# Capped attention and two feed-forward layers: the attention's waits re-ordered, the first inverse root moved from ScalarE and VectorE to a small Newton chain on GpSimd

## The chip, the core and the metric

The kernel runs on one core of one Trainium2 chip. The metric is device time in microseconds (us), lower is better. Before the change three runs took 539.45, 539.74 and 539.93 us, a median of 539.74 us. One further execution was profiled: it took 540.45 us, of which its instructions span 538.7 us. All times read below, and all positions ("at 69.76"), are microseconds from the start of that span.

The engines are named as the profile names them: PE is TensorE's matmul (PEld its weight load), DVE is VectorE, ACT is ScalarE, POOL is GpSimd, SP is SyncE, which here only issues DMAs.

## What is computed

```python
def _attn_ref(q, k, v, cap):                       # 2 batches x 12 heads x 448 x 64, float32
    scores = scale * np.matmul(q, k.transpose(0, 1, 3, 2))
    scores = cap * np.tanh(scores / cap)
    attn = np.exp(scores - np.max(scores, axis=-1, keepdims=True))
    attn = attn / (np.sum(attn, axis=-1, keepdims=True) + 1e-09)
    return np.matmul(attn, v)

def _moe_ref(x, w_gate, w_val, w_out, rms_g):      # 896 tokens, 768 wide, 1536 inside
    rms = np.sqrt(np.mean(x * x, axis=-1, keepdims=True) + 1e-06)
    xn = x / rms * rms_g
    g = xn @ w_gate
    return (g / (1.0 + np.exp(-g)) * (xn @ w_val)) @ w_out

def _moe2_ref(x, w_in, w_out, alpha):              # 896 tokens, 768 wide, 2048 inside
    h = x @ w_in
    return (np.maximum(h, 0.0) + alpha * np.minimum(h, 0.0)) @ w_out
```

The three are applied one after the other. The change touches how the attention is ordered and how 1/rms is made for the first of the two batches.

## The kernel before

Tokens lie along the free axis (448 per batch), features along the partitions. The attention goes through twelve head pairs, one in each pass of a loop `for i in range(NPAIR)`; below, "pass 9" is the pass with i = 9. Every instruction is put on its engine's queue in the order in which the code is written, and each engine works its queue strictly in that order, so the code order is the schedule. Tiles come from pools; a tile whose pool has no free buffer waits until the last reader of the buffer's previous tile is done.

What pass i puts on PE: the last 64 keys' scores of pair i (`qk_tail`, L219), three groups of six score matmuls (`qk`, L229), then the work of the pair before, i-1: its tail products and row sums (`sums`, L272 and L290), and its products with the values (`pv`, L256). In passes 4, 6, 8 and 10 two matmuls (`spread`, L373) also bring the inverse row sums of two earlier pairs to all partitions. ACT does the tanh of four score tiles (L240) and one long exp (L243) in a pass.

DVE serves all others: it copies finished outputs out of PSUM (`evac_o`, `ee`, L320) and row sums (`evac_u`, `us`, L328), which SP then lays out as 64 rows of 28 values (`gt`, L331). `recip` (L338 to L343: `gf`, `th`, `tl`) inverts these and two SP DMAs send them back as rows (`r`, L346). DVE also splits the queries and keys of the next pair in a high and a low part (`prep`: `hi` L195, `lo` L196) and decodes weights for the first layer (`w_bits` L122, `w_lo` L143, some of `w_hi` L137). Lists named `first` and `second` (filled by `a(...)` and `z(...)`) hold, per pass, what is issued behind `soft(i)` and at the pass's end. POOL has the squares for the mean square (`square`, L353 to L361) and sums of weight blocks (`sum1` to `sum4`, L130).

Two PSUM pools matter: `ps_o` (tag "o") and `ps_r` (tag "u") have one buffer each. The outputs `oo` of a pair, one of the two `spread` results, and the mean square `ms` of a batch share "o" in turn. The first batch's mean square is made in pass 9 by one matmul with ones (`rms_sum`, L398) of what POOL accumulated in six squares; DVE copies it to `spare` (L572), ACT takes the root of its mean (L405), which loads another table before and again behind it, and DVE inverts it in pass 10 (L408). The last pass' row sums and outputs (`us`, `oo`) share one PSUM tile.

Behind the attention both layers multiply 2 x 2 blocks by seven products (`P1` to `P7`) in slots; hooks `do(n, rank, fn)` put the work of ACT, DVE and POOL behind slot n, ordered by rank. `osplit` and `osplit_low` (L672 on DVE) split the operands of the first layer's output product, whose matmuls are L796.

Of the kernel before, what the change touches and what calls it, by code (L numbers as in the profile page):

```python
# [12 lines left out]
U32 = mybir.dt.uint32  # L13
AF = mybir.ActivationFunctionType
# [3 lines left out]
P = 128  # L18
# [39 lines left out]
def attn_moe_kernel(ctx: ExitStack, tc: tile.TileContext, units, qk_in, v, sel, w, gvec, alpha, out):  # L58
# [23 lines left out]
    r2 = [aconst.tile([P, S], F32R, name=f"r2_{i}") for i in range(2)]  # L82

# [193 lines left out]
    def sums(i):  # L277

        t = pt[i]
        if i == last:  # L280
            both = ps_s.tile([P, 2, 512], F32, tag="s", name="us")
            us[i], oo[i] = both[:, 0], both[:, 1]
        else:
            us[i] = under()
            if i:
                oo[i] = upper("oo")

        def add(h, x, k, m=slice(0, P), src=None):
            q = h + 2 * x
            nc.tensor.matmul(  # L290
                us[i][q * Q:q * Q + Q, HALF[0]], ones[m, :Q], t[m, k, src or HALF[x]], start=k == 2 * TG,
                stop=k // 2 == TG - 1, skip_group_check=True,
            )

        pv_tail(i, False)
        for h in range(2):
            for x in range(2):
                if split[i]:
                    add(h, x, 2 * TG, HEAD[x], HALF[h])
                else:  # L300
                    add(h, x, 2 * TG, HEAD[h])
        if i == 0 and split[i]:
            pv_tail(i, True)
        for n in range(2 * TG):
            for x in range(2):
                add(n % 2, x, n)
        if i and split[i]:
            pv_tail(i, True)
# [101 lines left out]

    oper = {}
# [56 lines left out]
    with tc.manual_schedule():  # L468
# [8 lines left out]
        for t in r2:  # L477
            nc.vector.memset(t.bitcast(F32), 0.0)
# [34 lines left out]
        def a(i, fn, *args):  # L513
            first.setdefault(i, []).append((fn, args))
# [3 lines left out]

        conv = conv_seq[:]
# [6 lines left out]
        for i in range(NPAIR):  # L526
# [6 lines left out]
            if i % 2 == 1 and i > 2:  # L533
                steps.insert(i < 9, (recip, (i - 3) // 2))
            for step in steps:
                a(i, *step)
            if i - 2 in range(len(conv)):
                a(i, w_bits, conv[i - 2])
                if i - 2 < len(conv) - RAW:
                    a(i, w_next, conv[i - 2])  # L540
# [8 lines left out]
        a(9, rms_root, 0)  # L549
# [4 lines left out]
        for put, n, fn, g in ((z, 6, sum1, 0), (z, 7, sum1, 1), (z, 7, sum2, 0), (a, 8, sum2, 1), (a, 8, sum3, 0),  # L554
                              (z, 8, sum3, 1), (z, 10, sum4, 0)):
            put(n, fn, "g", g)
        z(10, rms_tail, 0)
        a(11, xnorm, K3)
        z(11, xnorm, K3 + 1)
        for i in range(NPAIR):  # L560
# [8 lines left out]
            if i == 9:  # L569
                rms_sum(0, upper("ms"))  # L570
                rms_keep(0)
                nc.vector.tensor_copy(rstd[0], ms_of[0][:, :S])  # L572
                ms_of[0] = rstd[0]
            two = lambda: ps_s.tile([P, 2, 512], F32, tag="s", name="s")
            for g in range(TG - 1):
                qk(i, g, two())
                if pairs and i != 8 and g == 0:
                    norms(i - 4, under(), upper("rps"))
                if (i, g) == (1, 0):
                    oo[0] = upper("oo")  # L580
                    pv(0, range(2))
# [5 lines left out]
            if i == 10:  # L587
                sums(i - 1)
# [5 lines left out]
            if i and i != 10:  # L594
                sums(i - 1)
            if i == 1:
                evac_o(0)
            if i:
                evac_u(i - 1)
                if i > 1:  # L600
                    pv(i - 1)
                del pt[i - 1], hi[i - 1], lo[i - 1], vt[i - 1]
# [472 lines left out]
        for way, p, js, hi_at, lo_at in (  # L1075
# [5 lines left out]
            for h, j in enumerate(js):  # L1081
                do(o0 + hi_at[h], 0.2, osplit, way, p, j, h)
                do(o0 + lo_at[h], 2.2, osplit_low, way, p, j, h)
# [264 lines left out]
```

## Time and profile before

| what | value |
|---|---|
| median of three runs | 539.74 us |
| profiled execution: time, span | 540.45 us, 538.7 us |
| PE busy in the span | 530.2 us (98%) |
| PEld, DVE, ACT, POOL busy | 451.1, 448.2, 400.6, 112.0 us |
| PE busy from 60 to 80 us, from 80 to 100 us | 18.35, 19.16 us of 20 each |
| PE busy from 100 to 200 us, from 300 to 500 us | 100.0 us, 200.0 us |
| mean granted TensorE clock | 0.999 |

The attention takes the first hundred microseconds; behind it PE is hardly ever without work. So what the change can move lies in PE's holes of the first hundred microseconds, and in one hole behind them. An engine's busy time includes the time in which an instruction has begun and is held up, so a long instruction on DVE or POOL is compared with its usual length before it is called work. In a row of the timeline the first two columns are the start and the duration, both in us, x is the number of instructions, and what stands in brackets is the idle time before it with what ended it.

### The profile page before, as it was taken

To read this page: it belongs to the slowest core of one execution; us is meant where nothing else is said; L and a number is where in the kernel's file an instruction comes from. 1 tells how busy PE (TensorE), PEld (TensorE's weight loads), DVE (VectorE), ACT (ScalarE), POOL (GpSimd) and SP (SyncE) were. 2 spreads that over 40 slices of the span, in tenths; PEclk is the share of its full clock that TensorE was granted. 3 is DMA by queue.
4 is the path that set the end of the run, shared out by engine and by line. 5 is a ranking of instruction groups with operands and counts; after the bars stand their busy time and mean duration, and the time that the engine had idled before them with its cause. 6 is when DMAs were issued, how large, how long until landed. Compare 5 with 4: busy or idle time off the path is not lost.

```text
span 538.7 us, 8345 instructions
## 1 busy us (share of the span) xinstructions
PE 530.2 (98%) x3322; PEld 451.1 (84%) x3322; DVE 448.2 (83%) x516; ACT 400.6 (74%) x475; POOL 112.0 (21%) x80
## 2 busy tenths in 40 slices
PE   8999999999999999999999999999999999999997
PEld 5554544699999999999998999999999999999996
DVE  5588889798999968689779796869997897998951
ACT  7989989476766665477688776789989996995530
POOL 0023763300066441010013011110210231210000
PEclk9999999999999999999999999999999999999999
DMA  6856520400344426047865759433466789564111
GB/s 214 317 168 230 179 76 11 159 19 2 102 133 175 161 90 219 0 176 250 273 179 101 157 196 308 80 58 125 169 235 225 215 226 205 98 145 111 51 52 51
DMA packets 22343, 80.05 MB, mean 149 GB/s; under 512 B 3744, under 2 KB 6688, under 8 KB 22304
## 3 DMA queue, kind: packets, MB, share of 16 engines
q1 hardware_dynamic: 16378, 65.43, 35.4%
q0 software_dynamic: 5552, 13.70, 13.9%
q8 instruction: 26, 0.43, 0.3%
q10 hardware_dynamic: 374, 0.39, 0.2%
q14 instruction: 13, 0.11, 0.1%
HBM read 62.99 MB, written 2.75 MB: 122 GB/s over the span
## 4 chain that ended last, share of the span: by engine, by line
PE 88%; DVE 5%; ACT 3%; POOL 2%; DMA 1%; issue 1%; DVEq 0%; SPq 0%; ACTq 0%
PE s L450 19%; PE x L450 13%; PE m L450 13%; PE s L826 8%; PE x L826 7%; PE x L796 5%; PE s L796 5%; PE m L826 4%; PE m L796 3%; PE s L229 2%; PE oo L256 2%; PE rps L290 2%; PE s L462 1%; ACT pt L243 1%; DVE wt L122 1%; PE oo L272 1%
## 5 line engine op out<-in xcount | busy, mean ns | idle before, releaser
L143 DVE TENSOR_TENSOR wl<-wt,wh 128x768 fp32r<-128x768 f32 x109 | 111.5, 1024 | 21.2 <-ACT wh L137 20.8
L137 ACT CAST wh<-wt 128x768 fp32r<-128x768 f32 x106 | 87.7, 830 | 39.7 <-PE s L826 9.2
L130 POOL TENSOR_TENSOR wt<-wt 128x768 f32<-128x768 f32 x25 | 58.4, 2341 | 164.7 <-DVE wl L143 75.7
L117 ACT CAST top<-raw 128x768 f16<-128x768 bf16 x64 | 68.9, 1077 | 21.1 <-DMA raw<-w_in 11.6
L122 DVE SCALAR_TENSOR_TENSOR wt<-raw,top 128x768 uint32<-128x768 uint32 x64 | 66.8, 1045 | 1.0 <-ACT top L117 1.0
L450 PE MATMUL s<-xx,wh 128*128 128x448 f32 x264 | 63.6, 365 | 0.0
L672 DVE TENSOR_TENSOR xx<-b,xx 128x896 fp32r<-128x896 f32 (+1 forms) x55 | 62.1, 1135 | 0.0
L450 PEld LDWEIGHTS s<-xx,wh 128*128 128x128 f32 x264 | 49.3, 187 | 4.8 <-issue 0.9
L450 PE MATMUL x<-xx,wh 128*128 128x448 f32 x204 | 49.9, 366 | 0.0
L450 PE MATMUL m<-xx,wh 128*128 128x448 f32 x204 | 49.5, 364 | 0.0
L893 POOL DMA_DIRECT2D wt<-wt x25 | 21.6, 864 | 126.6 <-DVE wt L122 62.0
L240 ACT ACTIVATE pt<-s,cinv 128x896 f32<-128x896 f32 (+1 forms) x48 | 40.8, 910 | 5.0 <-PE s L229 2.4
L450 PEld LDWEIGHTS x<-xx,wh 128*128 128x128 f32 x204 | 38.2, 188 | 3.5 <-issue 0.4
L450 PEld LDWEIGHTS m<-xx,wh 128*128 128x128 f32 x204 | 38.3, 188 | 3.0
L826 PE MATMUL s<-xx,wh 128*128 128x448 f32 x144 | 40.5, 362 | 0.0
L826 PE MATMUL x<-xx,wh 128*128 128x448 f32 x128 | 36.0, 362 | 0.0
L243 ACT ACTIVATE pt<-pt,cap_t 128x3136 f32<-128x3136 f32 (+2 forms) x13 | 35.2, 2711 | 0.4
L450 PE MATMUL s<-xx,wl 128*128 128x448 f32 x132 | 33.8, 364 | 0.0
L796 PE MATMUL s<-xx,wh 128*128 128x448 f32 x108 | 30.4, 362 | 0.0
L826 PEld LDWEIGHTS s<-xx,wh 128*128 128x128 f32 x144 | 27.0, 187 | 2.3
L796 PE MATMUL x<-xx,wh 128*128 128x448 f32 x96 | 27.3, 363 | 0.6 <-DVE xx L672 0.6
L256 PE MATMUL oo<-pt,vt 128*32 128x448 f32 x264 | 27.1, 540 | 0.4 <-ACT pt L243 0.4
(208 smaller groups left out, 1124.7 us busy)
## 6 DMA issues: line engine op xcount, KB each, us to landing
raw<-w_in SPq DMA_DIRECT2D x68, 768.0 KB
wt<-wt POOLq DMA_DIRECT2D x25, 384.0 KB, 5.3
rw<-qk_in SPq DMA_DIRECT2D x11, 480.0 KB
vt<-v_in SPq DMA_DIRECT2D x12, 288.0 KB
lent<-wt POOLq DMA_DIRECT2D x5, 384.0 KB, 7.0
b<-b POOLq DMA_DIRECT2D x4, 448.0 KB, 5.3
out<-P SPq DMA_DIRECT2D x5, 224.0 KB
out<-b SPq DMA_DIRECT2D x2, 448.0 KB
```

The lines of the kernel that those rows point to most:

```text
L117: copy(top_of[u].bitcast(F16)[:, 1::2], raw_t[u].bitcast(BF16)[:, 4:4 * n + 4:4])
L122: nc.vector.scalar_tensor_tensor(out=f_t[u].bitcast(U32), in0=raw_t.pop(u).bitcast(U32)[:, 1:2 * n + 1:2], scalar=13, in1=top_of.pop(u), o ...
L130: add(out=t, in0=f_t[a], in1=f_t[b], op=op)
L137: copy(h_t[u], f_t[u].rearrange("p (k m) -> p k m", m=P))
L143: nc.vector.tensor_tensor(out=l_t[u], in0=f_t[u].rearrange("p (k m) -> p k m", m=P), in1=h_t[u], op=ALU.subtract)
L240: nc.scalar.activation(out=part, in_=st.pop((i, g)), func=AF.Tanh, scale=cinv)
L243: nc.scalar.activation(out=t[:, done:to], in_=t[:, done:to], func=AF.Exp, scale=cap_t)
L256: nc.tensor.matmul(oo[i][q * Q:q * Q + Q, :S], vv[:, n, q % 2 * Q:q % 2 * Q + Q], t[:, n, :], start=i == c == 0, stop=i > 0 and c == TG - ...
L450: nc.tensor.matmul(ps[:, r, :S], lhs, rhs, start=first and n == 0, stop=n == len(mm) - 1, skip_group_check=True,)
L672: nc.vector.tensor_tensor(out=out, in0=a, in1=b, op=op)
L796: nc.tensor.matmul(dst[m], wt[:, kk * MB + m, :], x, start=first and u == 0 and kk == 0 and n == 0, stop=u == UO - 1 and kk == 1 and n == ...
L826: nc.tensor.matmul(dst[m], wt[:, kk * MB + m, :], x, start=first and u == kk == i == 0, stop=last and kk == 1 and i == 2, skip_group_check ...
```

## The change

There are six edits.

1. `recip` now stands ahead of `prep` in passes 3, 5 and 7 too.
2. In passes 4, 6 and 8 the row sums of the pair before are copied out (and their DMAs issued) ahead of the weight decoding instead of behind it.
3. One weight sum on POOL (`sum2` of block 0) moves from ahead of the squares of pass 8 to behind them.
4. The first mean square: its matmul goes behind the first score group of pass 9. Instead of the copy to `spare`, ACT's root and DVE's inversion, DVE copies 32 rows to `mrow` at the end of the list `first[9]`, SP lays one row out as 16 x 28 values, POOL scales them, DVE makes a first guess of the inverse root with two integer operations, POOL runs four Newton steps of four operations and splits the result in two parts, four SP DMAs write them as rows of `rr`, and in pass 11 a matmul with `sel_t` spreads them; DVE copies that to `spare`.
5. In pass 10 the row sums go back behind all three score groups; in the last pass `us` and `oo` have a PSUM tile each.
6. In the first layer's output product the low part of one operand (`P6`, first half) is made one slot earlier and ranked ahead of more of the other work.

```diff
-            both = ps_s.tile([P, 2, 512], F32, tag="s", name="us")
-            us[i], oo[i] = both[:, 0], both[:, 1]
+            us[i], oo[i] = (ps_s.tile([P, 2, 512], F32, tag="s", name=x)[:, 0] for x in ("us", "oo"))
...
+    def root_begin(ms):
+        u = sb.tile([Q, S], F32, tag="sq", name="mrow", bufs=2)
+        nc.vector.tensor_copy(u, ms[:Q, :S])
+        nc.sync.dma_start(out=tiny_tile("x"), in_=u[:1].rearrange("h (p s) -> h p s", p=RP))
+
+    def root_small():
+        x, y, t = small["x"], tiny_tile("y"), tiny_tile("t")
+        ts, mul = nc.gpsimd.tensor_scalar, lambda o, a, b: nc.gpsimd.tensor_tensor(out=o, in0=a, in1=b, op=ALU.mult)
+        ts(out=x, in0=x, scalar1=1.0 / DM, scalar2=RMS_EPS, op0=ALU.mult, op1=ALU.add)
+        nc.vector.tensor_scalar(
+            out=t.bitcast(U32), in0=x.bitcast(U32), scalar1=1, scalar2=None, op0=ALU.logical_shift_right
+        )
+        nc.vector.tensor_scalar(
+            out=y.bitcast(I32), in0=t.bitcast(I32), scalar1=-1.0, scalar2=float(0x5F3759DF), op0=ALU.mult, op1=ALU.add
+        )
+        for _ in range(4):
+            mul(t, y, x)
+            mul(t, t, y)
+            ts(out=t, in0=t, scalar1=-0.5, scalar2=1.5, op0=ALU.mult, op1=ALU.add)
+            mul(y, y, t)
+        th, tl = tiny_tile("th", F32R), tiny_tile("tl", F32R)
+        nc.gpsimd.tensor_copy(th, y)
+        nc.gpsimd.tensor_tensor(out=tl, in0=y, in1=th, op=ALU.subtract)
+        for r0, part in enumerate((th, tl)):
+            for r in (r0, r0 + Q):
+                nc.sync.dma_start(
+                    out=rr[r:r + 1].rearrange("r (p s) -> r p s", p=RP).bitcast(F32), in_=part.bitcast(F32)
+                )
+
+    def root_end(ps):
+        nc.tensor.matmul(ps[:, :S], sel_t[:D], rr, start=True, stop=True, skip_group_check=True)
+        rms_keep(0)
+        nc.vector.tensor_copy(rstd[0], ps[:, :S])
...
+        EARLY = (4, 6, 8)
...
-                steps.insert(i < 9, (recip, (i - 3) // 2))
+                steps.insert(0, (recip, (i - 3) // 2))
             for step in steps:
                 a(i, *step)
             if i - 2 in range(len(conv)):
+                if i in EARLY:
+                    a(i, sums, i - 1)
+                    a(i, evac_u, i - 1)
                 a(i, w_bits, conv[i - 2])
...
-        a(9, rms_root, 0)
+        a(9, lambda: root_begin(ms_of.pop(0)))
+        z(9, root_small)
...
-        for put, n, fn, g in ((z, 6, sum1, 0), (z, 7, sum1, 1), (z, 7, sum2, 0), (a, 8, sum2, 1), (a, 8, sum3, 0),
+        for put, n, fn, g in ((z, 6, sum1, 0), (z, 7, sum1, 1), (a, 8, sum2, 0), (a, 8, sum2, 1), (a, 8, sum3, 0),
                               (z, 8, sum3, 1), (z, 10, sum4, 0)):
             put(n, fn, "g", g)
-        z(10, rms_tail, 0)
...
-            if i == 9:
-                rms_sum(0, upper("ms"))
-                rms_keep(0)
-                nc.vector.tensor_copy(rstd[0], ms_of[0][:, :S])
-                ms_of[0] = rstd[0]
...
+                if (i, g) == (11, 0):
+                    root_end(upper("rps"))
+                if (i, g) == (9, 0):
+                    rms_sum(0, upper("ms"))
...
-            if i == 10:
-                sums(i - 1)
             if i:
                 qk(i, TG - 1, third())
...
-            if i and i != 10:
+            if i and i not in EARLY:
                 sums(i - 1)
...
-                evac_u(i - 1)
+                if i not in EARLY:
+                    evac_u(i - 1)
...
-            (2, "P5", (4, 4, 0), (2, 3, 5), (4, 5, 6)), (0, "P6", (5, 5, 0), (5, 6, 8), (8, 8, 9)),
+            (2, "P5", (4, 4, 0), (2, 3, 5), (4, 5, 6)), (0, "P6", (5, 5, 0), (5, 6, 8), (7, 8, 9)),
...
-                do(o0 + lo_at[h], 2.2, osplit_low, way, p, j, h)
+                do(o0 + lo_at[h], 1.5 if (p, h) == ("P6", 0) else 2.2, osplit_low, way, p, j, h)
```

What stands in DVE's queue in pass 9 before the change, from the copy of pair 7's output (`ee`) to the copy of pair 8's row sums (`us`); `spare` is the copy of the mean square `ms`, `gf` to `tl` is `recip`, `hi` and `lo` are pair 10's:

```order
L320 COPY ee_958<-oo_916 128x448
L572 COPY spare_967<-ms_965 128x448
L338 TENSOR_SCALAR gf_1000<-gt_836,eps_t_87 64x28
L339 RECIPROCAL gf_1000<-gf_1000 64x28
L342 CAST th_1003<-gf_1000 64x28
L343 TENSOR_TENSOR tl_1004<-gf_1000,th_1003 64x28
L195 CAST hi_1009<-rw_896 128x832
L196 TENSOR_TENSOR lo_1010<-rw_896,hi_1009 128x832
L122 SCALAR_TENSOR_TENSOR wt_1013<-raw_703,top1_94 128x768
L328 COPY us_1043<-rps_1016 128x224
```

The same place after the change; `mrow` is now the copy that frees the PSUM buffer of `ms`, and `t` and `y` are the first guess:

```order
L321 COPY ee_960<-oo_906 128x448
L339 TENSOR_SCALAR gf_1000<-gt_838,eps_t_87 64x28
L340 RECIPROCAL gf_1000<-gf_1000 64x28
L343 CAST th_1003<-gf_1000 64x28
L344 TENSOR_TENSOR tl_1004<-gf_1000,th_1003 64x28
L197 CAST hi_1009<-rw_897 128x832
L198 TENSOR_TENSOR lo_1010<-rw_897,hi_1009 128x832
L124 SCALAR_TENSOR_TENSOR wt_1013<-raw_735,top1_95 128x768
L421 COPY mrow_1015<-ms_974 32x448
L329 COPY us_1046<-rps_1019 128x224
L429 TENSOR_SCALAR t_1063<-x_1017 16x28
L432 TENSOR_SCALAR y_1062<-t_1063 16x28
```

The copy out of `ms` moved from ahead of `recip` to behind `recip`, `prep` and the decoding of a weight block.

POOL's queue before, from the first block's S2 sum to the third weight sum behind the squares (`s2` is the accumulated square, `wt` a weight block):

```order
L130 TENSOR_TENSOR wt_312<-wt_754,wt_312 128x768
L357 TENSOR_TENSOR sq_906<-xf_95 128x448
L361 TENSOR_TENSOR s2_546<-s2_546,sq_906 128x448
L357 TENSOR_TENSOR sq_909<-xf_95 128x448
L361 TENSOR_TENSOR s2_546<-s2_546,sq_909 128x448
L130 TENSOR_TENSOR wt_406<-wt_853,wt_406 128x768
L130 TENSOR_TENSOR wt_500<-wt_701,wt_312 128x768
L130 TENSOR_TENSOR wt_605<-wt_807,wt_406 128x768
```

POOL's queue after, the same stretch up to the first operation on the small tile `x`:

```order
L358 TENSOR_TENSOR sq_937<-xf_96 128x448
L362 TENSOR_TENSOR s2_548<-s2_548,sq_937 128x448
L358 TENSOR_TENSOR sq_940<-xf_96 128x448
L362 TENSOR_TENSOR s2_548<-s2_548,sq_940 128x448
L132 TENSOR_TENSOR wt_314<-wt_756,wt_314 128x768
L132 TENSOR_TENSOR wt_408<-wt_855,wt_408 128x768
L132 TENSOR_TENSOR wt_532<-wt_733,wt_314 128x768
L132 TENSOR_TENSOR wt_607<-wt_809,wt_408 128x768
L428 TENSOR_SCALAR x_1017<-x_1017 16x28
```

One weight sum changed sides: four of them now stand in a row between the last square and the small chain.

PE's queue in pass 9 after the change, from the tail scores (L221) to the first matmul into pair 8's `oo`:

```order
L221 MATMUL s<-rw 64x224 x4
L231 MATMUL s<-hi 128x448 x2
L231 MATMUL s<-hi,lo 128x448 x2
L231 MATMUL s<-lo,hi 128x448 x2
L399 MATMUL ms<-s_548,ones 128x448
L231 MATMUL s<-hi 128x448 x2
L231 MATMUL s<-hi,lo 128x448 x2
L231 MATMUL s<-lo,hi 128x448 x2
L231 MATMUL s<-hi 128x448 x2
L231 MATMUL s<-hi,lo 128x448 x2
L231 MATMUL s<-lo,hi 128x448 x2
L274 MATMUL oo<-pt,vt 32x224 x4
```

The matmul into `ms` moved behind the first of the three score groups; the next tile in its buffer is still `oo`.

## Rows read from the trace of the kernel before

**Rows 1.** The page: PE's busy tenths in 40 equal slices of the span.

```profile
PE   8999999999999999999999999999999999999997
```

**Rows 2.** Timeline of PE, passes 7 and 8: start, duration, line, tiles, [idle before].

```profile
53.33 0.61 PE L219 MATMUL s<-rw 64*64 64x224 f32 x8
...
60.35 0.61 PE L219 MATMUL s<-rw 64*64 64x224 f32 x8
61.52 0.47 PE L373 MATMUL rps<-r,sel_t 64*128 64x448 f32 x2 [0.56 <-DMA r<-tl]
```

**Rows 3.** Timeline of PE, passes 9 to 11 and the last pair's products.

```profile
69.76 1.02 PE L398 MATMUL ms<-s,ones 128*128 128x448 f32 x2 [0.95 <-POOL s L361]
...
72.73 0.39 PE L272 MATMUL oo<-pt,vt 64*32 64x224 f32 x4
...
77.18 0.61 PE L219 MATMUL s<-rw 64*64 64x224 f32 x8
...
78.44 0.92 PE L373 MATMUL rps<-r,sel_t 64*128 64x448 f32 x2
...
85.51 0.61 PE L219 MATMUL s<-rw 64*64 64x224 f32 x8
...
87.76 0.47 PE L229 MATMUL s<-hi 64*128 64x448 f32 x2 [0.21 <-ACT pt L240]
...
96.18 2.46 PE L256 MATMUL us<-pt,vt 128*32 128x448 f32 x24 [0.51 <-DVE us L328]
```

**Rows 4.** Timeline of DVE in passes 7 and 8.

```profile
58.96 0.18 DVE L343 TENSOR_TENSOR tl<-gf,th 64x28 fp32r<-64x28 f32 x1
...
60.49 0.62 DVE L320 COPY ee<-oo 128x448 f32<-128x448 f32 x1 [0.18 <-PE oo L256]
```

**Rows 5.** Timeline of DVE in pass 9.

```profile
68.34 0.63 DVE L320 COPY ee<-oo 128x448 f32<-128x448 f32 x1 [0.34 <-PE oo L256]
70.81 0.62 DVE L572 COPY spare<-ms 128x448 f32<-128x448 f32 x1 [1.85 <-PE ms L398]
...
71.96 1.35 DVE L342 CAST th<-gf 64x28 fp32r<-64x28 f32 x1
73.35 1.76 DVE L343 TENSOR_TENSOR tl<-gf,th 64x28 fp32r<-64x28 f32 x1
75.03 0.58 DVE L195 CAST hi<-rw 128x832 fp32r<-128x832 f32 x1
75.64 1.03 DVE L196 TENSOR_TENSOR lo<-rw,hi 128x832 fp32r<-128x832 f32 x1
76.59 0.95 DVE L122 SCALAR_TENSOR_TENSOR wt<-raw,top 128x768 uint32<-128x768 uint32 x1
```

**Rows 6.** Timeline of POOL in passes 8 and 9.

```profile
63.69 1.28 POOL L357 TENSOR_TENSOR sq<-xf 128x448 f32<-128x448 f32 x1
...
68.57 1.14 POOL L361 TENSOR_TENSOR s<-s,sq 128x448 f32<-128x448 f32 x1
69.66 5.41 POOL L130 TENSOR_TENSOR wt<-wt 128x768 f32<-128x768 f32 x3
```

**Rows 7.** Busy time by stretch (PE, PEld, DVE, ACT, POOL), then PEclk, at the end.

```profile
535.00:536.00 1.00, 0.06 (x1) 0.00 (x0) 0.69 (x2) 0.00 (x0) 0.00 (x0) 1.00 0.61 224
...
537.00:538.00 1.00, 0.00 (x0) 0.00 (x0) 0.00 (x0) 0.00 (x0) 0.00 (x0) 0.93 0.12 38
538.00:538.67 0.67, 0.00 (x0) 0.00 (x0) 0.00 (x0) 0.00 (x0) 0.00 (x0) 0.50 0.00 0
```

**Rows 8.** Timeline of PE at the start.

```profile
1.06 3.35 PE L473 MATMUL warm<-ones 128*128 128x128 f32 x14 [1.06 <-DVE ones L470]
4.41 0.74 PE L229 MATMUL s<-hi 64*128 64x448 f32 x2
...
5.57 0.36 PE L229 MATMUL s<-hi 64*128 64x448 f32 x2
```

**Rows 9.** Timeline of PE in the first layer's output product.

```profile
287.48 0.47 PE L796 MATMUL x<-xx,wh 128*128 128x448 f32 x1 [0.63 <-DVE xx L672]
```

More of the change, by code (lines that the diff above doesn't have):

```diff
@@ L13 @@
 U32 = mybir.dt.uint32
+I32 = mybir.dt.int32
 AF = mybir.ActivationFunctionType
@@ L82, in attn_moe_kernel @@
     r2 = [aconst.tile([P, S], F32R, name=f"r2_{i}") for i in range(2)]
+    rr = aconst.tile([D, S], F32R, name="rr")
     UW = UK * P
@@ L408, in rms_tail, with tiny_tile @@
         nc.vector.reciprocal(out=rstd[b], in_=rstd[b])
+    small = {}
+    def tiny_tile(name, dt=F32):
+        small[name] = aconst.tile([RP, S // RP], dt, name=name)
+        return small[name]
+    def root_begin(ms):
[29 more added lines that the diff above has]
+        nc.vector.tensor_copy(rstd[0], ps[:, :S])
     oper = {}
@@ L476, in attn_moe_kernel @@
             nc.vector.memset(t, 0)
-        for t in r2:
+        for t in (*r2, rr):
             nc.vector.memset(t.bitcast(F32), 0.0)
```

## The prediction

> **What bounds the kernel now.** I read the page first: PE's slices are full from the eighth on and only nearly full before [rows 1], so the time is PE's queue plus its holes, and the holes lie in the attention. Then PE's timeline, for the price of each hole. A pass without one takes 7.02 us from tail scores to tail scores (53.33 to 60.35) [rows 2]. Pass 8 waits 0.56 for an inverse row sum, pass 9 waits 0.95 for POOL's squares, pass 10 takes 8.33 (77.18 to 85.51), pass 11 waits 0.21 for ACT, the last pair's value products wait 0.51 for DVE [rows 2, 3]; behind the attention only 0.63 is left, in the first layer's output product [rows 9]. The change aims at all of these. Last I read DVE and POOL in pass 9, because the first thing that the new order does there is to make PE wait for DVE.
>
> **The early edits.** With row sums sent off ahead of a weight decode (0.95 [rows 5]) and inverted ahead of `prep`, pass 8's spread no longer waits for its DMA. What is late next is the copy of pair 6's output, whose PSUM buffer the spread takes: it ends at 60.49 + 0.62 = 61.11 [rows 4]. The spread starts at about 61.1 instead of 61.52 [rows 2]: 0.4 gained, or nothing if the inversion itself now waits for its row sums. The zeroing of `rr` lies beside DVE's wait for the first load; without that cover it is one copy of 448 columns, 0.6 [rows 5].
>
> **Pass 9, the term that decides.** Pair 8's products go into the single PSUM buffer of `ms`, so they wait for the copy out of `ms`. That copy stood directly behind the matmul (70.81 [rows 5]). Now it is `mrow`, behind `recip`, `prep` and a weight decode, and PE can't pass it: row sums, value products and all of pass 10 stand behind it.
>
> When is `mrow` done? Unhindered: pair 7's output copy ends at 68.97 - 0.4 = 68.6 [rows 5]; four small operations of about 0.25 make 1.0 (estimated above the 0.18 of `tl` [rows 4]), `hi` 0.58, `lo` 1.03, decode 0.95 [rows 5], the copy about 0.45 (32 rows of the 0.62 kind): 72.6. But the same small operations took 1.35 and 1.76 in pass 9 of the trace [rows 5], and they end at 73.31 and 75.11, just where the second and third of POOL's weight sums end (69.66 + 5.41 = 75.07 in three of 1.80 [rows 6]). So DVE's cast and its two-input subtraction each stand until POOL's running sum is over, and POOL gets in its next one ahead of DVE's next one. `hi`, behind POOL's last sum, took its plain 0.58.
>
> Now POOL has four sums there, not three, and DVE comes to `recip` as they begin, since it no longer waits 1.85 for `ms` [rows 5]. The squares can start when pair 4 is scaled: 61.1 + 0.47 for the spread [rows 2] + 0.62 = 62.2. They need 6.0 as before (63.69 to 69.71 [rows 6]): 68.2. Then `th` waits for the first sum (70.0), `tl` for the second (71.8), `hi` for the third (73.6), holding the fourth up by 0.45, and `lo` for the fourth: 73.6 + 0.45 + 1.8 = 75.9. Add `lo` 1.03, decode 0.95, copy 0.45, less 0.3 for overlapping ends: 78.0.
>
> PE would be there at 72.73 - 0.4 - 0.95 = 71.4 (the wait for POOL is gone, since the squares end at 68.2, while a score group stands ahead of the `ms` matmul now). So the products start at 78.0 instead of 72.73 [rows 3]: **+5.3**, with a hole of 6.6. The bounds are 72.6, no hindrance at all, which is -0.1, and 78.7, if DVE comes a step later, +6. I take the value next to rows 5 and 6, which show the same instructions against the same kind of sum.
>
> **What is gained behind it.** Pass 10: DVE was late there, so the two spreads ran one behind the other (0.92 for the pair against 0.47 [rows 2, 3]) and the row sums cut the scores in two. With DVE ahead of the delayed PE the pass is 7.02 + 0.25 for the spreads instead of 8.33: **-1.05**. Pass 11: ACT loses two table loads and a root, its 0.21 goes; the new spread of `rr` costs one matmul, about 0.2: 0. The last pair: two PSUM tiles, **-0.5** [rows 3]; next late is the split of the operand for the first feed-forward product, which is done within that distance. Output product: the low part is made some four DVE operations earlier, so its 0.63 goes [rows 9]; DVE had the operand's high part early enough: **-0.6**. DVE loses a 448-column inversion in pass 10, off the path.
>
> **The small chain.** No row shows a 16 x 28 operation of POOL; bounds are 0 and 1.14 each (128 x 448 [rows 6]). A line through 1.14 at 448 and 1.80 at 768 columns gives 0.27 at 28; I take that, since the small size lies at the line's end. `x` lands at about 78.0 + 2.4 (from the end of `tl` at 59.14 to the spread at 61.52 took that [rows 2, 4]) = 80.4; DVE's first guess stands behind the row sums of pair 8, about 82; eighteen operations make 4.9: 87. The four DMAs, 2.4 and three further issues of 0.6 each, land at 91. PE wants them in pass 11: 78.0 + 4.45 (72.73 to 77.18 [rows 3]) + 7.3 + 1.25 = 91.0 at full clock, later if the clock falls. So hidden with nothing to spare: 0 taken, up to 3 if an operation costs 0.45. SP's load of the last values waits behind these DMAs, but is wanted ten microseconds later.
>
> **The clock.** At the end of the trace PE stops at 535.06 (0.06 of that slice busy), and the granted clock reads 0.93 for 537 to 538 and 0.50 behind: it fell from 2.4 to 1.2 GHz some 2.8 us into idleness [rows 7]. A hole of 6.6 is longer. At the start matmuls run from 1.06, and a 448-column pair still takes 0.74 at 4.41 but 0.36 at 5.57 [rows 8]: slow work for about 4.3 us, of which half is lost: **+2.1**. Bounds: 0, and 4.45 if all of pass 9's products ran at half speed.
>
> The Trainium skill (TensorE: Matmul & The Clock Gate, section "What's actually happening") says that half rate is the default and that only recent activity releases it; it speaks against any order that gathers PE's small waits into one hole. By that rule the sum is the one below; by the holes of up to 1 us in this trace, which left the clock's mean at 0.999, it would be 2.1 less. Rows 7 agree with the rule.
>
> **Sum.** 5.3 - 1.05 - 0.5 - 0.6 = +3.15 with the clock kept, +5.25 with the clock lost. The profiled execution took 540.45, so 545.7; it lies 0.7 above the median of 539.74, so the median goes to 545.0.
>
> **Rivals.** *The hole, but the clock holds*: +3.15, 542.9. For it: only the end of the trace shows a fall, and nothing ran after it. Against: 6.6 is far over 2.8. *No hindrance by POOL*: `mrow` at 72.6, the products at their old time, and all gains stay: -0.1 - 1.05 - 0.5 - 0.6 = -2.25, 537.5, faster than before. It decides from the point where `mrow` is done by 72.6, and is still faster than before up to about 74.7 (+2.0 and no loss of clock). For it: DVE is free early and its plain work is short. Against it: 1.35 and 1.76 for operations of 0.18. A half case, where DVE slips two operations into one of POOL's gaps, spares one or two sums of 1.8: a hole of 3 to 5, 540 to 543. *The small chain late*: 2 to 3 on top, 547.5. For it: no margin; against it: the lower clock gives PE's demand two microseconds more. *The change doesn't do what it says*: the earlier inversion idles DVE in pass 3 for its row sums, at most some tenths, inside the range.
>
> **How the numbers follow.** The forecast 0.55 (own range 543.7 to 546.8), the hole with the clock kept or a half case 0.20, the late chain 0.10, no hindrance 0.13, gains and hole cancelling 0.02. About 0.2% (1.1 us) is what a measurement of this kernel tells from no change. Faster 0.14, same 0.04, slower 0.82. The range reaches down through the half cases to 540.2 and up into the late chain to 547.5.
>
> **What would show it.** Right: PE idle for 5 to 8 us in pass 9, ended by DVE's `mrow`; `th`, `tl`, `hi`, `lo` long in that pass, each ending with one of POOL's four sums; a granted clock below 1.00 in the slices behind the hole; pass 10 at about 7.3; no hole at the last pair's products and in the output product. Wrong: `mrow` done near 72 to 73, or POOL's sums finished before DVE reaches `recip`; PE waiting in pass 11 for a DMA of `rr` instead.

## The result, and the profile after

The changed kernel takes 545.28 us (median of four runs, 544.94 to 545.83) against 539.68 of the kernel before in the same set (539.45 to 539.93): a ratio of 1.0105, with an interval of 1.0092 to 1.0118. So it is slower by 1.05%, 0.3 us beside the forecast. The profiled execution took 545.83 us with a span of 544.0; the span grew by 5.3. (In the changed file the lines of the code around the attention stand one to two lower, those of the first layer's product 44: L219 is now L221, L229 L231, L256 L258, L272 L274, L290 L291, L373 L374, L450 L494.)

The slices of the page, first PE's busy time, then the granted clock in tenths. Before, PE was full from the eighth on [rows 1], and the page had 9 for the clock in all forty:

```profile
PE   8999959999999999999999999999999999999997
...
PEclk9999979999999999999999999999999999999999
```

PE's timeline of the attention, as in [rows 2, 3] (start, duration, engine, line, operation, tiles, form, count, and in brackets the idle time ahead with what ended it):

```profile
60.95 0.61 PE L221 MATMUL s<-rw 64*64 64x224 f32 x8
61.49 0.74 PE L374 MATMUL rps<-r,sel_t 64*128 64x448 f32 x2
68.43 0.61 PE L221 MATMUL s<-rw 64*64 64x224 f32 x8
...
78.51 0.60 PE L274 MATMUL oo<-pt,vt 64*32 64x224 f32 x4 [6.29 <-DVE mrow L421]
...
82.02 2.43 PE L258 MATMUL oo<-pt,vt 128*32 128x448 f32 x24
84.38 0.61 PE L221 MATMUL s<-rw 64*64 64x224 f32 x8
...
85.63 0.36 PE L374 MATMUL rps<-r,sel_t 64*128 64x448 f32 x2
...
91.68 0.61 PE L221 MATMUL s<-rw 64*64 64x224 f32 x8
...
93.70 0.44 PE L450 MATMUL rps<-rr,sel_t 64*128 64x448 f32 x1 [0.61 <-DMA rr<-tl]
...
102.19 2.44 PE L258 MATMUL oo<-pt,vt 128*32 128x448 f32 x24
104.56 0.98 PE L494 MATMUL s<-xx,wh 128*128 128x448 f32 x3
```

One hole of 6.29 us stands in pass 9, and it ends with DVE's `mrow`. The spread of pass 8 no longer waits, the two spreads of pass 10 (85.63) run together, and the last pair's value products (102.19) follow at once. A new wait of 0.61 for `rr` stands in pass 11. Behind the attention the profile shows no wait of PE at all, where 0.63 stood [rows 9].

From tail scores to tail scores the passes compare as follows (starts of L219 and L221, the last spreads at 93.01 and 99.71, the first product at 98.57 and 104.56):

| stretch | before | after | difference |
|---|---|---|---|
| up to pass 4 | 31.45 | 31.68 | +0.23 |
| pass 4, 5 | 7.30, 7.27 | 7.95, 7.01 | +0.65, -0.26 |
| pass 6, 7 | 7.31, 7.02 | 7.31, 7.00 | 0.00, -0.02 |
| pass 8 | 7.85 | 7.48 | -0.37 |
| pass 9 | 8.98 | 15.95 | +6.97 |
| pass 10 | 8.33 | 7.30 | -1.03 |
| pass 11 | 7.50 | 8.03 | +0.53 |
| last pair | 5.56 | 4.85 | -0.71 |
| behind it, to the end | 440.13 | 439.44 | -0.69 |
| sum | 538.7 | 544.0 | +5.3 |

The +0.23 is there from the first pass on and comes from the first microseconds, where the clock rose later: a pair of 448 columns took 0.36 at 5.57 before [rows 8], and 0.58 still at 5.74 now. Of the edits only the zeroing of `rr` acts there, and it doesn't explain this: in the profiles of the experiments, which all have it, the first tail scores start anywhere from 7.15 to 7.80 (7.17 before, 7.40 here). Why `mrow` is late is read from DVE in pass 9, to be laid beside [rows 5]:

```profile
69.11 1.31 DVE L339 TENSOR_SCALAR gf<-gt,eps_t 64x28 f32<-64x28 f32 x1
...
70.82 1.42 DVE L343 CAST th<-gf 64x28 fp32r<-64x28 f32 x1
72.27 1.73 DVE L344 TENSOR_TENSOR tl<-gf,th 64x28 fp32r<-64x28 f32 x1
73.92 0.58 DVE L197 CAST hi<-rw 128x832 fp32r<-128x832 f32 x1
74.53 2.52 DVE L198 TENSOR_TENSOR lo<-rw,hi 128x832 fp32r<-128x832 f32 x1
76.98 0.94 DVE L124 SCALAR_TENSOR_TENSOR wt<-raw,top 128x768 uint32<-128x768 uint32 x1
77.85 0.60 DVE L421 COPY mrow<-ms 32x448 f32<-32x448 f32 x1
```

and from POOL, to be laid beside [rows 6]:

```profile
68.55 7.63 POOL L132 TENSOR_TENSOR wt<-wt 128x768 f32<-128x768 f32 x4
82.18 0.21 POOL L428 TENSOR_SCALAR x<-x 16x28 f32<-16x28 f32 x1 [6.00 <-DMA x<-mrow]
...
87.87 0.94 POOL L438 TENSOR_SCALAR t<-t 16x28 f32<-16x28 f32 x1
```

POOL's four sums run from 68.55 to 76.18. `gf`, `th` and `tl` each last until one of them ends (70.4, 72.2, 74.0); `hi` slips in ahead of the fourth with its plain 0.58; `lo` stands until the fourth ends at 76.18 and then takes 0.87 more, to 77.05. The inversion between `gf` and `th` (L340) ran in 0.32 beside a sum, as it does alone. The clock by stretches (length, busy time with the number of instructions of PE, PEld, DVE, ACT and POOL, then the granted clock, the DMA share and GB/s; cut to the stretches around the hole):

```profile
73.00:74.00 1.00, 0.00 (x0) 0.00 (x0) 1.00 (x2) 0.97 (x2) 1.00 (x2) 1.00 0.05 7
74.00:75.00 1.00, 0.00 (x0) 0.00 (x0) 0.97 (x2) 1.00 (x1) 1.00 (x1) 0.89 0.00 0
75.00:76.00 1.00, 0.00 (x0) 0.00 (x0) 1.00 (x1) 1.00 (x1) 1.00 (x1) 0.50 0.05 7
...
80.00:81.00 1.00, 1.00 (x20) 0.47 (x14) 0.00 (x0) 0.00 (x0) 0.00 (x0) 0.50 0.00 0
81.00:82.00 1.00, 1.00 (x20) 0.56 (x16) 0.11 (x1) 0.00 (x0) 0.00 (x0) 0.70 0.00 0
82.00:83.00 1.00, 1.00 (x18) 0.36 (x12) 0.83 (x4) 0.00 (x0) 0.27 (x2) 1.00 0.00 0
```

The clock falls from 2.4 to 1.2 GHz in the hole, near 74.8, and rises again near 81.6 (the means 0.89 and 0.70 are of microseconds that lie partly at either level). So pair 8's tail products and row sums take 82.02 - 78.51 = 3.51 us instead of 74.81 - 72.73 = 2.08 [rows 3, 5].

### The profile page after: what moved, and what is told of

It is laid out like the page before. It is cut to its first block, busy times and chain, and to the rows that moved or that the text cites. A ratio compares the mean times of both kernels' runs of the same rounds, so it can differ in the third digit from the quotient of the medians.

```text
span 544.0 us, 8375 instructions
## 1 busy us (share of the span) xinstructions
PE 531.6 (98%) x3323; PEld 452.2 (83%) x3323; DVE 447.1 (82%) x519; ACT 398.6 (73%) x472; POOL 117.2 (22%) x99
## 4 chain that ended last, share of the span: by engine, by line
PE 91%; DVE 3%; DMA 2%; ACT 1%; POOL 1%; issue 1%; SPq 0%; DVEq 0%; POOLq 0%
PE s L494 19%; PE x L494 13%; PE m L494 13%; PE s L873 8%; PE x L873 7%; PE s L843 6%; PE x L843 5%; PE m L873 4%; PE oo L258 3%; PE s L231 3%; PE m L843 3%; PE rps L291 2%; PE oo L274 1%; PE s L506 1%; DMA gt<-us 1%
## 5 line engine op out<-in xcount | busy, mean ns | idle before, releaser
L124 DVE SCALAR_TENSOR_TENSOR wt<-raw,top 128x768 uint32<-128x768 uint32 x64 | 65.7, 1029 | 0.8 <-ACT top L119 0.8
L494 PE MATMUL s<-xx,wh 128*128 128x448 f32 x264 | 63.8, 365 | 0.0
L494 PEld LDWEIGHTS s<-xx,wh 128*128 128x128 f32 x264 | 49.3, 187 | 5.0 <-DVE xf L466 0.7
L494 PE MATMUL x<-xx,wh 128*128 128x448 f32 x204 | 49.9, 366 | 0.0
L494 PE MATMUL m<-xx,wh 128*128 128x448 f32 x204 | 49.5, 364 | 0.0
L494 PEld LDWEIGHTS x<-xx,wh 128*128 128x128 f32 x204 | 38.2, 188 | 3.5 <-issue 0.4
L494 PEld LDWEIGHTS m<-xx,wh 128*128 128x128 f32 x204 | 38.2, 187 | 3.0
L494 PE MATMUL s<-xx,wl 128*128 128x448 f32 x132 | 33.8, 364 | 0.0
L258 PE MATMUL oo<-pt,vt 128*32 128x448 f32 x288 | 29.5, 540 | 0.4 <-ACT pt L245 0.3
```

The lines of the kernel that those rows point to most:

```text
L124: nc.vector.scalar_tensor_tensor(out=f_t[u].bitcast(U32), in0=raw_t.pop(u).bitcast(U32)[:, 1:2 * n + 1:2], scalar=13, in1=top_of.pop(u), o ...
L258: nc.tensor.matmul(oo[i][q * Q:q * Q + Q, :S], vv[:, n, q % 2 * Q:q % 2 * Q + Q], t[:, n, :], start=i == c == 0, stop=i > 0 and c == TG - ...
L494: nc.tensor.matmul(ps[:, r, :S], lhs, rhs, start=first and n == 0, stop=n == len(mm) - 1, skip_group_check=True,)
```

## The experiments

The theory: the time is lost because `mrow`, which alone frees the PSUM buffer for pair 8's products, stands behind DVE operations that POOL's sums hold up; the lost clock comes on top. The rivals: POOL's extra sum, or the small chain, costs the time by itself. All times are beside the kernel before (539.6 to 540.1 us in these sets); ratios are to it.

**1. mrow at once.**

```
                 if (i, g) == (9, 0):
                     rms_sum(0, upper("ms"))
+                    root_begin(ms_of.pop(0))
...
-        a(9, lambda: root_begin(ms_of.pop(0)))
```

> The only difference from the changed kernel: mrow is copied directly behind the mean square's matmul, ahead of recip, prep and the weight decode (and its DMA is issued ahead of the next loads). My theory, that the loss is mrow's place on DVE: pair 8's products start at about 72.2 instead of 78.5 (-6.3), the clock stays at full speed in pass 9 (-1.4, the sums taking 2.08 again instead of 3.5), and DVE, still held up by POOL's four sums, is now late in pass 10 as it was before the change (the spreads wait up to 1.7 and go one behind the other, +1.9): about 539.5 us. Rival A, the sums of POOL or the small chain cost the time wherever mrow stands: the hole only moves to pass 10 or 11, 542 or more. Rival B, nothing is late behind it: 537.6.

Measured: 542.78 us (540.71 to 544.6), 1.0051 (1.0032 to 1.007). PE in its pass 10 and 11:

```profile
77.87 0.47 PE L374 MATMUL rps<-r,sel_t 64*128 64x448 f32 x1 [0.49 <-DVE us L329]
79.14 0.47 PE L374 MATMUL rps<-r,sel_t 64*128 64x448 f32 x1 [0.80 <-DVE ee L321]
...
88.99 0.44 PE L450 MATMUL rps<-rr,sel_t 64*128 64x448 f32 x1 [0.88 <-DMA rr<-tl]
```

The hole of pass 9 is gone: products at 71.45 without a wait, the row sums in 2.08. So the place of that one copy made it. But the time did not come down to 539.5. DVE, with the four sums still on it, is late in pass 10 (the two waits above, as expected), `rr` is late by 0.88, and the clock falls here too, which I had not expected of waits this short (last section). Each run has a mean clock of 0.994 to 0.997; the lowest belongs to the longest run. So the theory holds for the hole, but the time is rival A's: by the medians half of what was lost moved on to passes 10 and 11. The profiled execution, at 541.04 us, is among the fastest of the six; that the others lost up to 3.6 us more by the same waits and falls of the clock is likely, but no trace shows it.

**2. Three sums behind the squares, not four.**

```
-(z, 7, sum1, 1), (a, 8, sum2, 0)
+(z, 7, sum1, 1), (z, 7, sum2, 0)
```

> The only difference from the changed kernel: POOL's sum2 of block 0 goes back ahead of the squares of pass 8, so that three weight sums stand behind them, not four. My theory: the hole is made by mrow's place, and the fourth sum only decides which of DVE's operations is held up; the squares end a microsecond later, so the three sums end at nearly the same time as the four do now, lo runs at its plain 1.03, and the products start between 77.5 and 78.5: 544.3 to 545.3 us. Rival, the fourth sum is a cause of its own: the hole is shorter by its 1.8, 543.4 us or less.

Measured: 543.99 us, 1.0085 (1.0072 to 1.0098), between the two expectations.

```profile
77.27 0.60 PE L274 MATMUL oo<-pt,vt 64*32 64x224 f32 x4 [5.53 <-DVE mrow L421]
...
81.19 2.82 PE L258 MATMUL oo<-pt,vt 128*32 128x448 f32 x24
```

The hole shrinks by 0.76 only, and `rr` is no longer late. `lo` was not at its plain 1.03: it took 2.52 again, held by the third sum, while `gf` had got through in 0.54. So the fourth sum is a cause of its own for 0.8 of the 6.3, not for 1.8, and the hole stays without it. Even these 0.8 are not gained: the clock stood at 0.50 until about 82.0 here too, so more of pair 8's products ran at it (the value products took 2.82, not 2.43), and pass 9 took 15.98 us, as long as with four sums (15.95). What the profile gains lies in pass 4 (7.30 for 7.95, see the next section) and in pass 11, where the wait for `rr` is gone.

**3. The four sums behind the small chain.**

```
-(a, 8, sum2, 0), (a, 8, sum2, 1), (a, 8, sum3, 0), (z, 8, sum3, 1)
+(z, 9, sum2, 0), (z, 9, sum2, 1), (z, 9, sum3, 0), (z, 9, sum3, 1)
```

> The only difference from the changed kernel: POOL's four weight sums stand behind its small chain, at the end of pass 9, and mrow stays behind recip, prep and the decode. My theory, that DVE's operations in pass 9 are long only because POOL's sums hold them up: th, tl, hi and lo take 0.17, 0.18, 0.58 and 1.03, mrow is done at about 72.9 and the products start at 73.0, a hole of 0.8 instead of 6.3, and the clock keeps its full speed: 537.6 to 538.5 us, unless the sums come too late for the first layer's products at 98 (then some microseconds more there, to be seen as a wait of PE behind the attention). Rival, DVE is slow in pass 9 for another reason (its operands, the loads that run beside it): th to lo stay near their 1.4 to 2.5, about 545 us.

Measured: 545.75 us, 1.0111 (1.0098 to 1.0124). DVE in pass 9, and then `gf` of pass 11:

```profile
68.86 0.17 DVE L343 CAST th<-gf 64x28 fp32r<-64x28 f32 x1
69.07 0.18 DVE L344 TENSOR_TENSOR tl<-gf,th 64x28 fp32r<-64x28 f32 x1
69.17 0.58 DVE L197 CAST hi<-rw 128x832 fp32r<-128x832 f32 x1
69.79 1.03 DVE L198 TENSOR_TENSOR lo<-rw,hi 128x832 fp32r<-128x832 f32 x1
...
89.18 3.64 DVE L339 TENSOR_SCALAR gf<-gt,eps_t 64x28 f32<-64x28 f32 x1 [0.79 <-DMA gt<-us]
```

POOL beside that last `gf`:

```profile
83.85 7.16 POOL L132 TENSOR_TENSOR wt<-wt 128x768 f32<-128x768 f32 x4
...
91.86 0.92 POOL L358 TENSOR_TENSOR sq<-xf 128x448 f32<-128x448 f32 x1
```

PE in pass 9 and at the last pair:

```profile
72.26 0.39 PE L274 MATMUL oo<-pt,vt 64*32 64x224 f32 x4 [0.89 <-DVE mrow L421]
...
97.69 0.71 PE L374 MATMUL s<-r,sel_t 64*128 64x448 f32 x1 [4.29 <-DMA r<-tl]
```

Pass 9 went to the letter: the same operations at their plain lengths, a hole of 0.89. That shows that POOL's sums made them long. The time failed, at a place that I had not looked at: the sums now ran from 83.85 to 91.01, on the last inversion of row sums in pass 11. `gf` took 3.64 instead of 0.23: it stood not through one operation of POOL but through three, the last sum and the two squares behind it, and ended at 92.82, as the second square did (92.78). PE waited 4.29 for the DMA behind it, the clock fell again, and `rr` was late by 1.9. So the sums cost microseconds at both places where a short DVE operation on PE's path stood beside them.

**4. PE kept busy in the hole.**

```
+        if i == 8:
+            for _ in range(24):
+                nc.tensor.matmul(us[i][:, :P], ones, ones, start=True, stop=True, skip_group_check=True)
         pv_tail(i, False)
```

> The only difference from the changed kernel: 24 matmuls of ones with ones (the form of the warm-up at the start, into the tile of the row sums, which are then written over) stand on PE ahead of pair 8's tail products, where it is idle for 6.3 us; nothing else is done with them. My theory: the hole stays and ends at 78.5, but the granted clock stays at full speed in it, and pair 8's row sums take 2.08 instead of 3.5: 1.4 less, 543.9 us. As the prediction had it, 2.1 less: 543.2 us. Rival, the clock costs nothing here: 545.3 us.

Measured: 543.64 us, 1.0071 (1.0059 to 1.0083).

```profile
71.44 5.62 PE L298 MATMUL rps<-ones 128*128 128x128 f32 x48
77.81 0.39 PE L274 MATMUL oo<-pt,vt 64*32 64x224 f32 x4 [0.74 <-DVE mrow L424]
...
78.05 1.64 PE L291 MATMUL rps<-pt,ones 64*32 64x224 f32 x28
```

The clock stays at 1.00, the products follow at full speed (79.89 - 77.81 = 2.08), and pass 9 takes 14.52 us instead of 15.95. The gain is 1.6 us by the medians, 1.8 by the ratios. So the clock's share of the loss is 1.4 by the trace of pass 9 and at most 1.8 by the times, not the 2.1 of the prediction and not nothing.

**5. The sums spread out, three Newton steps.** As the first, and besides:

```
-(a, 8, sum2, 0), (a, 8, sum2, 1), (a, 8, sum3, 0), (z, 8, sum3, 1)
+(z, 7, sum2, 0), (a, 8, sum2, 1), (z, 9, sum3, 0), (z, 10, sum3, 1)
...
-        z(9, root_small)
+        a(9, root_small)
...
-        for _ in range(4):
+        for _ in range(3):
```

> From the changed kernel: mrow directly behind the mean square's matmul; POOL's four weight sums of pass 9 spread out (one ahead of pass 8's squares, one behind them, one behind the small chain, one behind pass 10's squares); the small chain ahead of pair 8's row sums, and three Newton steps instead of four. My theory, that the change's other edits do gain and only mrow's place and the crowd of POOL's sums against DVE cost the time: no hole in pass 9 (products at about 71.5, no later than 72.2), pass 10 at 7.3, no wait for rr, the clock at full speed throughout. Against the kernel before: pass 8 -0.4, pass 9 -0.8, pass 10 -1.0, pass 11 -0.2, last pair -0.7, output product -0.7: about 536 us. Rival A, DVE stays late in pass 10 whatever the sums do (then waits of the spreads as in the first experiment and a fall of the clock): 539 to 542. Rival B, rr is late still: a wait of up to 1 in pass 11, 537.

Measured: 539.35 us, 0.9989 (0.998 to 0.9997). No hole in pass 9, pass 10 in 7.34, `rr` in time. One wait is left, at the last pair:

```profile
92.44 0.44 PE L374 MATMUL s<-r,sel_t 64*128 64x448 f32 x1 [1.78 <-DMA r<-tl]
```

Neither rival was right. SP issued the four DMAs of `rr` from 80.54 to 83.20 and only then those of the row sums, which `gf` awaited until 87.61; then one more sum held `th` for 1.42. The time fell short of the expected 536 by more than this wait: the profiled execution took 538.98, and its first product stands at 97.29, 1.3 earlier than before the change. Beside the wait, the first passes start 0.4 later there than before the change, and the stretch behind the first product is only 0.2 shorter, not 0.7.

**6. The old root**, with the copy to `spare` behind the matmul, the root on ACT and the inversion on DVE; all other edits of the change stay.

```
                     rms_sum(0, upper("ms"))
+                    rms_keep(0)
+                    nc.vector.tensor_copy(rstd[0], ms_of[0][:, :S])
+                    ms_of[0] = rstd[0]
...
-        a(9, lambda: root_begin(ms_of.pop(0)))
-        z(9, root_small)
+        a(9, rms_root, 0)
+        z(10, rms_tail, 0)
-                if (i, g) == (11, 0):
-                    root_end(upper("rps"))
```

> From the changed kernel: the mean square's root is made as before the change (copy to spare directly behind its matmul, root on ACT, inversion of 448 columns on DVE in pass 10); all other edits stay, the place of the matmul and POOL's four sums among them. It is the first experiment without the small chain. Theory, that the small chain has no cost of its own beyond its late rr: pass 9 without a hole, DVE late in pass 10 as in the first experiment with the same waits (0.5 and 0.8) and fall of the clock, no wait for rr in pass 11: 0.9 less than that, about 541 us (540 to 542.5). Rival, the small operations of POOL are what makes DVE late: below 539.

Measured: 538.31 us, 0.997 (0.9959 to 0.998): faster than the kernel before, where I had expected 541. The number is the rival's, but not its mechanism: DVE is late in pass 10 with nearly the waits of the first experiment (0.50 and 0.53, for 0.49 and 0.80). What my theory missed is that the clock held here. So the change's other edits together gain 0.3%. The same order with the small chain (experiment 1) is 4.5 us slower by the medians; by their profiles 2.2, of which 1.65 lie in pass 10, where the clock fell, and the wait for `rr` is the next largest part.

**7. The old root and the sums spread out** (the edits on the root from 6, those on the sums from 5).

> As the version with the sums spread out, but with the old root (copy to spare behind the matmul, root on ACT, inversion on DVE in pass 10). Theory: what matters is the order, not the form of the root, so this is within 1 us of the version with the small chain (536 to 537.5 us): the inversion's 2.94 on DVE and ACT's two table loads lie beside PE's work. Rival, the small chain itself gains: this one waits for ACT in pass 11 and for DVE behind the inversion, 538 or more.

Measured: 538.27 us (537.64 to 539.72), 0.9969 (0.9958 to 0.998), 1.1 less than with the small chain, but short of the theory's 537.5. DVE is in time in pass 10; now ACT is late there, with the root (0.67) and two table loads (1.28 each) ahead of its tanh, much as the rival had it for pass 11. The profiled execution is the slowest of the seven (539.72):

```profile
79.97 0.47 PE L231 MATMUL s<-hi 64*128 64x448 f32 x2 [1.67 <-ACT pt L242]
...
81.02 2.81 PE L291 MATMUL rps<-pt,ones 64*32 64x224 f32 x28
```

**8. Two sums behind the squares, the chain earlier.** As 5, but `(a, 8, sum3, 0)` and `(z, 9, sum3, 1)`, and `root_small` directly behind `prep`.

> From the version with the sums spread out: a second of POOL's weight sums behind pass 8's squares (where POOL idles 3.5 us for x), one behind the small chain, and DVE's first guess directly behind prep. Theory, that the only wait left there (1.8 at the last pair's spread, for the inverse row sums) is DVE's th held up by a weight sum in pass 11, behind row sums whose DMA stood in SP's queue behind the four DMAs of rr: th runs at its plain 0.17, the wait shrinks to 0.5 or less, and the time is 538 us, 1.3 less than that version. Rival, the wait is the DMA queue's alone: it stays at 1.5 or more, 539.3.

Measured: 538.76 us, 0.9976 (0.9966 to 0.9987). `th` ran in 0.17 and the wait at the last pair fell to 0.57, nearly as the theory had it (by the profile it now ends with a cast of ACT); but five of the chain's operations took 0.60 to 0.98 beside DVE's (0.87, 0.69, 0.60, 0.98 and 0.80), and `rr` came 0.85 late:

```profile
86.12 0.44 PE L450 MATMUL rps<-rr,sel_t 64*128 64x448 f32 x1 [0.85 <-DMA rr<-tl]
```

This is the best version with the small chain: faster than the kernel before by 0.24%.

**9. The old root behind pass 10's exp.** As 7, with `a(10, rms_root, 0)`.

> As the version with the old root and the sums spread out, but ACT takes the root in pass 10 behind its own tanh and exp, not ahead of them. Theory: the wait of PE for ACT in pass 10 (1.7) and the fall of the clock behind it go; pass 10 takes 7.3, DVE's inversion runs beside it, nothing is late in pass 11: 536.5 us (536 to 537). Rival, the root's table loads now delay pass 11's tanh, or the inversion delays the copy of pair 9's outputs: a wait of 1 to 2 there, 538.

Measured: 540.14 us (538.75 to 541.0), 0.9996 (0.9986 to 1.0005). The rival was right about the waits, both of them: PE's wait for ACT, now 1.86, only moved one pass on, and the inversion then delayed the copy of pair 9's outputs by 0.64. Its time of 538 was 2 too low, though: in most runs, the profiled one among them, the clock fell behind these waits (last section).

**10. The late edits undone.** As 6, with `both` for the last pair and the old slot and rank of the low part.

> As the version with the old root, but the last pair's row sums and outputs share one PSUM tile again, and the output product's low part has its old slot and rank. Theory, that these two edits each gain what the traces show: the last pair's stretch on PE is longer by 0.7 and the wait of 0.6 in the output product is back: 538.3 + 1.4 = 539.7 us. Rival, DVE now has both done early anyway: 538.3.

Measured: 539.48 us, 0.9999 (0.999 to 1.0007). The last pair's wait of 0.51 is back and its stretch is longer by 0.72 (5.56 for 4.84). But no wait is back in the output product, and the stretch behind the first product is no longer than in experiment 6 (439.14 for 439.37). So the profiles show 0.7 for the last pair, while what the output product's edit does stays open: the medians differ by 1.2. Without these two edits the rest of the re-ordering shows no gain in time (0.9999).

**11. The copy late, with the old root.** As 6, but the copy to `spare` stands where the change has `mrow`:

```
+        def copy_late():
+            rms_keep(0)
+            nc.vector.tensor_copy(rstd[0], ms_of[0][:, :S])
+            ms_of[0] = rstd[0]
+
+        a(9, copy_late)
         a(9, rms_root, 0)
```

> As the version with the old root, but its copy out of the mean square's PSUM buffer (to spare) stands behind recip, prep and the weight decode, where the change has mrow; no small chain at all. Theory, that the place of that one copy makes the whole loss: a hole of 6 in pass 9, pair 8's products at about 78, half the clock for a few microseconds behind it, pass 10 at 7.3, no wait for rr: 544.4 us. Rival, the small chain has a part in the hole: 541 or less.

Measured: 545.47 us, 1.011 (1.0094 to 1.0126).

```profile
78.28 0.60 PE L274 MATMUL oo<-pt,vt 64*32 64x224 f32 x4 [6.26 <-DVE spare L601]
```

Without any small chain, the late copy alone makes the same hole (6.26 for 6.29), the same fall of the clock and the same time. Against experiment 6 that is 7.2 us by the medians (7.6 by the ratios) for the place of one instruction of 0.6.

## Why the prediction was right

The forecast of 545.0 and its mechanism hold. That the sum came out within 0.3 is partly luck, since terms were off in opposite directions: the products' start and pass 11 by 0.5 us each upwards, the clock by 0.7, the last pair by 0.2 and the output product by 0.1 downwards.

- **Pass 9.** Forecast: products at 78.0, a hole of 6.6, ended by `mrow`; measured 78.51, of which 0.23 come from the start of the trace, and 6.29. Experiments 1 and 11 show that the copy's place makes it, experiment 3 that POOL's sums make the copy late. One detail was off: I had the sums hold `th`, `tl`, `hi` and `lo`; it was `gf`, `th`, `tl` and `lo`. I took `gf` to be free, since it ran in 0.22 before, at 71.36; there the running sum was almost over (69.66 + 1.82 = 71.48). The Trainium skill (SBUF — State Buffer, section "Who interferes with whom") counts one-input scalar operations, copies and casts among those that can take the pair of ports shared with GpSimd, and says that the one who comes second waits for the whole of the other; the trace agrees, with 1.31 for `gf` here, up to the end of POOL's first sum. In experiment 3 the wait was longer than that: 3.64, through three operations of POOL.
- **The clock.** Forecast 2.1, measured 1.4 in pass 9, 1.6 to 1.8 by the times (experiment 4). The step that was mis-sized is the length of slow work: 4.3 us taken from the start of the trace, some 3.1 here (from 78.51 to about 81.6).
- **Early edits.** -0.4 for pass 8 came as -0.37. But I had nothing for pass 4, which lost 0.65, while pass 5 gained 0.26. In the profiled execution the inversion, now ahead of `prep`, idled 2.12 us for its row sums, so the copy that the spread needs came late:

```profile
27.21 0.23 DVE L339 TENSOR_SCALAR gf<-gt,eps_t 64x28 f32<-64x28 f32 x1 [2.12 <-DMA gt<-us]
```

  This was my last rival, priced at some tenths. It varies: in the profiles of the experiments, with the same early edits, pass 4 took 7.30 to 7.58 and PE was not idle ahead of its spread, while pass 5 took 7.00 to 7.02 in all of them. So most of the 0.65 is this one execution's, and the 0.26 comes with the edits.
- **Gains behind it.** Pass 10 at 7.30 (forecast 7.27); last pair -0.71 (forecast -0.5: the wait of 0.51 and 0.2 around it that I left out); output product -0.69 (forecast -0.6), though experiment 10 does not tie that to its edit.
- **The small chain.** Forecast: hidden with nothing to spare, 0; measured +0.53 in pass 11, and 0.88 where the hole was gone (experiment 1). Mis-sized twice: `x` took 3.7 us to arrive (78.45 to 82.18), not 2.4, and the operations start 0.31 apart, not 0.27, with three of them taking 0.65 to 0.94 beside DVE's `hi`, `lo` and `wl`. The wait for `rr` in pass 11, which I had named as a sign of being wrong, did come, with 0.61, but beside the hole and not in its place.

## What to carry to other kernels

A copy that frees a single-buffer PSUM tile is on TensorE's path, however short it is: here one of 0.6 us, moved behind seven operations of its own engine, some of them held up, cost 7.2. Sums on GpSimd do not only cost their own time: here they held up VectorE's casts, its scalar operation and its two-input operations on SBUF tiles, each until a sum ended and once for longer, while its inversion (0.32) and its copies out of PSUM (`spare` 0.62 [rows 5]) ran beside them at their plain lengths. So such sums belong where no short VectorE operation of the first kinds is waited for, and moving them can merely move the loss (experiment 3). And a wait of TensorE is to be priced with what the clock loses behind it, here 1.4 to 1.8 us for a hole of 6.3.

## What the runs showed of the hardware

The clock fell after waits far shorter than the hole, too. In experiment 1 it fell within the microsecond 79 to 80, behind waits of 0.49 and 0.80 (columns as above):

```profile
78.00:79.00 1.00, 0.34 (x1) 0.05 (x1) 1.00 (x3) 0.43 (x1) 0.64 (x2) 1.00 0.00 0
79.00:80.00 1.00, 0.86 (x6) 0.80 (x8) 0.97 (x3) 0.00 (x0) 0.71 (x4) 0.82 0.03 4
80.00:82.00 2.00, 2.00 (x17) 1.22 (x21) 1.97 (x4) 1.26 (x2) 1.75 (x3) 0.50 0.00 0
```

In experiment 6, with waits of 0.50 and 0.53 at the same place, it held:

```profile
78.00:79.00 1.00, 0.46 (x1) 0.18 (x1) 1.00 (x3) 0.98 (x2) 0.00 (x0) 1.00 0.00 0
79.00:80.00 1.00, 0.69 (x6) 0.66 (x7) 0.97 (x3) 0.99 (x2) 0.14 (x1) 1.00 0.01 2
80.00:82.00 2.00, 2.00 (x37) 0.99 (x39) 1.97 (x3) 2.00 (x4) 2.00 (x2) 1.00 0.53 147
```

One wait of 1.67 was followed by a fall (experiment 7, where it came when PE was busy again: the row sums at 81.02 took 2.81 instead of 1.64), one of 1.78 was not (experiment 5). After 1.86 it fell in experiment 9 (0.55 for 88 to 89) and did not in experiment 3 (in pass 11, ahead of `rr`; 1.00 from 87 to 89). So waits of the same length were followed by a fall or not, and the same kernel did both from run to run: experiment 9's runs lie at 538.75 to 539.2 with a mean clock of 0.999 or 1.000 and at 539.8 to 541.0 with 0.997. The Trainium skill (TensorE: Matmul & The Clock Gate, section "What's actually happening") says that the chip's look at PE's activity runs freely, so that a change of clock falls at another point in each run; the spread of these runs agrees. A small operation of POOL (16 x 28 values) took 0.20 to 0.24 us, 0.31 from start to start.
